# Three early expert jobs after the seventh unit instead of two, and four weight loads moved behind the load of unit 8

## The chip, the cores and the metric

The kernel runs on one core of a Trainium2 chip. The metric is the device time of one execution in microseconds (us); lower is better. The engines are named as the profile names them: PE is TensorE (PEld its weight loads), DVE is VectorE, ACT is ScalarE, POOL is GpSimd, SP is SyncE. A "q" behind an engine's name (SPq, ACTq) marks its sequencer, which issues transfers.

## The reference

A gated scan over 4 sequences of 3648 tokens with 256 channels, and then a two-level mixture of experts over the 14592 resulting tokens. There are 4 groups of 4 experts, each expert a pair of matrices 256x1024 and 1024x256 with a relu between them; a token goes to one expert.

```python
sig = 1.0 / (1.0 + np.exp(-f_logit))
f = lower_bound + (1.0 - lower_bound) * sig
for t in range(S):
    h = f[:, t] * h + (1 - f[:, t]) * x[:, t]
    y[:, t] = h
# y, as N x 256, is the input x of the experts
g_idx = argmax(x @ w_group); g_w = softmax(x @ w_group)[g_idx]
e_idx = argmax(xg @ w_expert[g]); e_w = softmax(xg @ w_expert[g])[e_idx]
out[token] = g_w * e_w * (relu(xg @ w1[g, e]) @ w2[g, e])
```

## The kernel before

**Units.** The tokens are worked off in 29 units of 512 (the last has 256), numbered from 0, so "unit 8" is the ninth. `p1_load` (L174) brings a unit's 1 MB into one of four `zt` buffers; the loads of units 0 to 8 are issued by SP and those from unit 9 on by ACT (`ZX_SP = 9`). ACT computes the gate (tanh L184, affine L194), DVE the gated input (L210, L230) and the scan (`h`, L221, two per unit), PE the transposes back to rows (L248) and the router's logits (L262, L273). After each group of units (`GROUPS`: unit 0, units 1-2, 3-4, 5, 6, then pairs) the routing runs: DVE operations L283 to L377 with the exponential on ACT (L370 up to unit 6, L311 later), and at its end POOL scatters the group's rows, one transfer for 128 rows (L343), into the expert lists `xs` in HBM.

**Jobs.** An expert's tokens go through one early job ("A", in expert order) and one late job ("B", largest first). Early job e is described by `EARLY[e] = (u, n)`: when the units below u are routed, its last 128*n rows (or all, if there are fewer) are loaded from the list (`job_rows`, L750, by SP, behind the scatters). What is left of each expert goes into the late jobs, whose sizes in rows are fixed by `CAPS`, the largest first; a loop at the end takes rows above the caps. For a list that is too short at its cut, SP writes blank rows ahead of it (`early_blanks`, L534, 258 KB for n = 2), two units ahead of the cut's loads. `close_early` (L542, L544) notes what has been taken.

A job has four weight pieces of 512 KB (`job_weights`, L758, on SP, eight staging buffers), each split into a high and a low part (`job_split`: ACT cast L764, DVE subtraction L765); its rows are transposed (L805) and split (L810, L811); the first product runs on L839 to L841 (three matmuls for each block, relu and split on ACT L844 and DVE L845) and the second on L858, scaled on ACT L870 and scattered to the output by POOL (L871).

**Order.** All unit work is cut into 422 small steps (`thunks`), with a mark where a cut is reached: mark 7 at step 126, "begun" at 136, mark 9 at 181, mark 11 at 208, mark 13 at 235. Up to "begun" the steps and the first job's preparation are in the order written. In that stretch the weight pieces are placed by `EARLY_FETCH`: `(5, 4)` puts the first four pieces (job 0) behind the load of unit 5, `(7, 8)` the next four (job 1) behind the load of unit 7, all on SP, which issues strictly in the order written.

```python
for u, n in EARLY_FETCH:
    while u not in last_load:
        bg_pop()
    fetch_to(n)
```

After "begun" the jobs run one behind the other, and unit steps are put between their parts at a rate given by due times. A job of 256 rows counts 10 pieces of work (eight column blocks and two output tiles). The mark that job k+2 needs is due when half of job k is done; before job k+1 begins at PE, its own mark must have been reached. Within these priorities a planner with costs of its own orders each engine's instructions; SP keeps the written order.

```python
nxt = macros[mi + 2][0]
due.append((at - work(mac) // 2, marks[EARLY[nxt.idx][0]] if nxt.kind == "A" else marks["order"]))
```

Two places of the written order matter below. The load of unit 8 comes in SP's order behind the loads of units 6 and 7, the two blanks for cut 9, and job 1's four weight pieces. And in ACT's order the tanh of unit 8 stands ahead of the exponential and the row copies of unit 6's routing, which is the last routing before cut 7; then come the scatters of unit 6, and the loads of the rows for cut 7.

Of the kernel before, what the change touches and what calls it, by code (L numbers as in the profile page):

```python
# [19 lines left out]
NE = 16  # L20
UNIT = 512

EARLY = [(7, 2), (7, 2), (9, 2), (9, 2), (11, 2), (11, 2), (13, 3), (15, 3),
         (15, 3), (17, 4), (19, 4), (21, 4), (23, 5), (25, 5), (27, 6), (27, 6)]
CAPS = [848, 748, 724, 592, 588, 560, 528, 488, 464, 460, 448, 420, 392, 296, 168, 112]
EXTRA_AT = []
GROUPS = [1, 2, 2, 1, 1] + [2] * 11
LAG = 7
EARLY_FETCH = [(5, 4), (7, 8)]
STG_BUFS = 8  # L30
XR_BUFS = 6
ROW_BUFS = 6
# [2 lines left out]
AHEAD = 3  # L35
MT = -(-max(CAPS) // 128)
ZX_SP = 9
# [3 lines left out]
def gated_scan_moe(ctx: ExitStack, tc, zx, lower, wroute, wexp, out, S):  # L41
# [7 lines left out]
    NT = N // P  # L49
    PRE = max(n for _, n in EARLY) * P  # L50
    LW = PRE + N + 2 * P
# [34 lines left out]
    def iota_f32(name, shape, pattern, base=0, mult=0):  # L86
        t = const.tile([P] + shape, F32, name=name)
        nc.gpsimd.iota(t, pattern=pattern, base=base, channel_multiplier=mult,
                       allow_small_or_imprecise_dtypes=True)
        return t  # L90
# [6 lines left out]
    nc.gpsimd.tensor_copy(taken, eoff)  # L97
    cuts = {u for u, _ in EARLY}
    eidx = iota_f32("eidx", [NE], [[1, NE]])
# [97 lines left out]
    def p1_ta(u):  # L197
        p1_tanh(u)
        p1_affine(u)
# [186 lines left out]
    def p1_thunks(us, groups):  # L386
# [21 lines left out]
        def put(f):  # L408
            th.append(f or (lambda: None))
            if hasattr(f, "mark"):  # L410
                marks[f.mark] = len(th)

        put(lambda: [p1_load(u) for u in range(us[0], us[0] + AHEAD - 1)])
        put(lambda: p1_ta(us[0]))
        cut = EARLY[0][0]

# [12 lines left out]
        for u in us + [us[-1] + 1]:  # L429
# [58 lines left out]
            for t in seq:  # L488
                put(t)
                slot += 1  # L490
                for _ in range(2 if u <= EARLY[0][0] else 1):
                    if not hold:
# [37 lines left out]
    def early_blanks(u):  # L530
        for e, (v, n) in enumerate(EARLY):
            if v == u:
                r = e * LW + PRE - n * P
                sync.dma_start(out=xs_v[NT + e][r:r + n * P, :].rearrange("(p k) c -> p k c", k=n),  # L534
                               in_=blank[:, None, :].broadcast_to([P, n, RW]))

    def close_early(u):
        posA = rt.tile([P, NE], I32, name="posA")
        for n in sorted({m for v, m in EARLY if v == u}):
            es = [e for e, s in enumerate(EARLY) if s == (u, n)]  # L540
# [119 lines left out]
    for s in range(NE):  # L660
        nc.vector.memset(caps[:, s:s + 1], float(CAPS[s]))
    onesf = const.tile([P, NE], F32, name="onesf")
# [8 lines left out]
    def make_job(kind, idx):  # L671
        j = Job()
        j.kind, j.idx = kind, idx
        j.len = EARLY[idx][1] * P if kind == "A" else CAPS[idx] if kind == "B" else P
        j.tiles = -(-j.len // P)
# [297 lines left out]
    with tc.manual_schedule(engines={mybir.EngineType.PE, mybir.EngineType.DVE, mybir.EngineType.Activation}):  # L973
        for u, n in EARLY_FETCH:
            while u not in last_load:
# [99 lines left out]
```

## Time and profile before

| | |
|---|---|
| median of 3 runs | 781.0 us (780.71 to 781.51) |
| the profiled execution | 782.62 us |
| its span, first to last instruction | 780.9 us |
| PE busy in the span | 712.0 us (91%) |
| DVE busy | 538.5 us (69%) |
| ACT busy | 460.0 us (59%) |
| POOL busy | 289.7 us (37%) |
| mean granted TensorE clock | 0.964 |

The shares are means over stages that differ much: in the first 70 us there is nothing but unit work; then unit work and early jobs run side by side until all units are routed (about 281 us); then only jobs are left.

### The profile page before, as it was taken

Reading aid. Unit: us, or ns where it says so; the run is one execution under the profiler, and the core shown is the slowest. Engines: PE = TensorE matmul, PEld = TensorE weight load, DVE = VectorE, ACT = ScalarE, POOL = GpSimd, SP = SyncE. Lnnn points to the kernel's source line nnn. Section 1 sums busy time; section 2 is a strip of 40 time slices with the busy share of each in tenths; the row PEclk is TensorE's granted clock in tenths of the full one; section 3 lists DMA queues with packets and bytes.
Section 4 is the critical chain, followed back from the end, with each engine's and each line's share of the span. In section 5 each row is a group of like instructions: output and inputs, shape, how many; then the busy total and the mean of one; then the engine's idle time right before and its main releaser. Section 6 shows DMA issues by size and latency. Waiting matters only on the chain.

```text
span 780.9 us, 20863 instructions
## 1 busy us (share of the span) xinstructions
PE 712.0 (91%) x8112; PEld 631.9 (81%) x8112; DVE 538.5 (69%) x1058; ACT 460.0 (59%) x824; POOL 289.7 (37%) x272
## 2 busy tenths in 40 slices
PE   2653759999999989999999999999999999999995
PEld 1432547888988878889988898999999999999995
DVE  6869999999999976675654645546554676666640
ACT  6558767987878855445445445454455465555541
POOL 3662163677556453552112212223232222222232
PEclk9955969999999999999999999999999999999998
DMA  7997989899999935359355433553554465555300
GB/s 274 345 360 223 359 242 370 302 337 337 310 344 304 364 121 185 121 185 256 121 135 108 148 90 113 142 124 116 136 161 112 145 170 170 153 168 175 88 30 25
DMA packets 96005, 155.58 MB, mean 199 GB/s; under 512 B 52320, under 2 KB 64637, under 8 KB 92576
## 3 DMA queue, kind: packets, MB, share of 16 engines
q1 hardware_dynamic: 80928, 103.73, 45.0%
q0 software_dynamic: 11424, 30.02, 11.2%
q10 hardware_dynamic: 3552, 20.48, 7.2%
q8 instruction: 64, 1.05, 0.6%
q14 instruction: 37, 0.30, 0.1%
HBM read 112.69 MB, written 42.02 MB: 198 GB/s over the span
## 4 chain that ended last, share of the span: by engine, by line
PE 61%; DMA 10%; DVE 9%; issue 5%; ACT 3%; POOL 2%; SPq 1%; POOLq 0%; ACTq 0%; DVEq 0%
PE ps_m L858 29%; PE ps_m L839 7%; PE ps_m L840 7%; PE ps_m L841 7%; DVE wl L765 3%; PE ps_p L839 3%; PE ps_p L841 3%; PE ps_p L840 3%; DMA xs<-rows,posi 3%; DMA xr<-xs 2%; DVE h L221 2%; POOL out_dram L871 2%; DMA zt<-in_zx_dram 2%; DVE hl L845 1%; DMA out_dram<-o,meta 1%
## 5 line engine op out<-in xcount | busy, mean ns | idle before, releaser
L858 PE MATMUL ps_m<-wh,hh 128*128 128x256 f16 (+2 forms) x1320 | 265.8, 252 | 2.8 <-ACT hh L844 2.8
L858 PE MATMUL ps_m<-wh,hl 128*128 128x256 f16 (+2 forms) x1320 | 265.7, 251 | 1.7 <-DVE hl L845 1.6
L858 PE MATMUL ps_m<-wl,hh 128*128 128x256 bf16 (+2 forms) x1320 | 266.0, 251 | 0.1
L858 PEld LDWEIGHTS <-hh 128*128 128x128 f16 (+2 forms) x2640 | 195.6, 99 | 26.5 <-issue 3.3
L839 PE MATMUL ps_m<-xh,wh 128*128 128x256 f16 (+11 forms) x782 | 195.9, 261 | 3.5 <-DVE hl L845 3.5
L840 PE MATMUL ps_m<-xl,wh 128*128 128x256 bf16 (+11 forms) x782 | 196.1, 260 | 0.0
L841 PE MATMUL ps_m<-xh,wl 128*128 128x256 f16 (+11 forms) x782 | 195.9, 260 | 0.0
L765 DVE TENSOR_TENSOR wl<-st,wh 128x1024 bf16<-128x1024 f32 x128 | 154.1, 1217 | 51.4 <-ACT wh L764 51.2
L343 POOL DMA_INDIRECT xs<-rows,posi x114 | 132.9, 1166 | 126.5 <-issue 51.9
L871 POOL DMA_INDIRECT out_dram<-o,info x75 | 87.0, 1161 | 241.6 <-ACT o L870 213.3
L845 DVE SCALAR_TENSOR_TENSOR hl<-ps_m,hh 128x512 bf16<-128x512 f32 (+6 forms) x176 | 117.1, 668 | 73.4 <-ACT hh L844 72.9
L844 ACT ACTIVATE hh<-ps_m 128x512 f16<-128x512 f32 (+6 forms) x176 | 103.6, 590 | 73.0 <-PE ps_m L841 71.4
L764 ACT CAST wh<-st 128x1024 f16<-128x1024 f32 x128 | 132.3, 1048 | 13.9 <-PE ps_m L858 7.7
L840 PEld LDWEIGHTS <-wh 128*128 128x128 f16 x1088 | 106.9, 98 | 12.2 <-issue 4.6
L839 PEld LDWEIGHTS <-wh 128*128 128x128 f16 x1088 | 106.8, 98 | 10.6 <-issue 1.8
L858 PEld LDWEIGHTS <-hl 128*128 128x128 bf16 (+2 forms) x1320 | 104.5, 99 | 12.5 <-DVE hl L845 2.1
L841 PEld LDWEIGHTS <-wl 128*128 128x128 bf16 x1088 | 106.7, 98 | 7.8 <-issue 0.2
L871 POOL DMA_INDIRECT out_dram<-o,meta x55 | 65.3, 1188 | 115.7 <-ACT o L870 105.2
L870 ACT ACTIVATE o<-ps_m,info 128x256 f32<-128x256 f32 (+4 forms) x75 | 33.0, 441 | 84.3 <-PE ps_m L858 77.0
L839 PE MATMUL ps_p<-xh,wh 128*128 128x256 f16 (+13 forms) x306 | 73.3, 252 | 0.0
L840 PE MATMUL ps_p<-xl,wh 128*128 128x256 bf16 (+13 forms) x306 | 73.3, 252 | 0.0
L841 PE MATMUL ps_p<-xh,wl 128*128 128x256 f16 (+13 forms) x306 | 73.3, 252 | 0.0
(145 smaller groups left out, 738.2 us busy)
## 6 DMA issues: line engine op xcount, KB each, us to landing
st<-in_wexp_dram SPq DMA_DIRECT2D x128, 512.0 KB, 6.4
zt<-in_zx_dram ACTq DMA_DIRECT2D x19, 1024.0 KB, 9.4
zt<-in_zx_dram SPq DMA_DIRECT2D x7, 1024.0 KB, 10.0
xr<-xs SPq DMA_DIRECT2D x25, 258.0 KB, 4.9
xs<-blank SPq DMA_DIRECT2D x22, 258.0 KB, 4.6
xs<-rows,posi POOLq DMA_INDIRECT x114
xs<-blank SPq DMA_DIRECT2D x3, 516.0 KB
xs<-blank SPq DMA_DIRECT2D x2, 774.0 KB, 17.7
```

The lines of the kernel that those rows point to most:

```text
L221: nc.vector.tensor_tensor_scan(out=h[:, k, c0 - a:c1 - a], data0=ff[:, k, c0 - a:c1 - a], data1=uu[:, k, c0 - a:c1 - a], initial=init, op0 ...
L343: sc = nc.gpsimd.indirect_dma_start(out=xs_v[G["t0"] + t][:, :], out_offset=bass.IndirectOffsetOnAxis(ap=R["posi"][:, t:t + 1], axis=0), i ...
L764: nc.scalar.copy(j.wh[i], j.st[i])
L765: nc.vector.tensor_tensor(out=j.wl[i], in0=j.st[i], in1=j.wh[i], op=ALU.subtract)
L839: nc.tensor.matmul(po, w1_at(j.wh, k, c), xh[:, k], start=(k == 0), stop=False)
L840: nc.tensor.matmul(po, w1_at(j.wh, k, c), xl[:, k], start=False, stop=False)
L841: nc.tensor.matmul(po, w1_at(j.wl, k, c), xh[:, k], start=False, stop=(k == KD - 1))
L844: nc.scalar.activation(hi, pv, AF.Relu)
L845: nc.vector.scalar_tensor_tensor(out=j.hl[ch][:, cs[0]:cs[-1] + 1, 0:w], in0=pv, scalar=0.0, in1=hi, op0=ALU.max, op1=ALU.subtract)
L858: nc.tensor.matmul(pm[i * q:i * q + n, 0:dw], h[ch][:, c, ts], w2_at(w, c)[:, i * dw:(i + 1) * dw], start=(c == 0 and s == 0), stop=(c == ...
L870: nc.scalar.activation(o[s, 0:dw], pm[s, 0:dw], AF.Copy, scale=lt.bitcast(F32)[s, r, 1:2])
L871: nc.gpsimd.indirect_dma_start(out=out_v[out_n[0]].rearrange("n (g d) -> (n g) d", g=g), out_offset=bass.IndirectOffsetOnAxis(ap=lt[s, r, ...
```

## The change

Expert 2's early job moves from cut 9 to cut 7 and expert 4's from cut 11 to cut 9. So cut 7 feeds three jobs, cut 9 two (experts 3 and 4) and cut 11 one (expert 5); the number of rows that a job works on stays 256. The caps of the late jobs in slots 3 to 6 are set anew (592, 588, 560, 528 become 616, 592, 588, 548). And job 1's four weight pieces are issued behind the load of unit 8 instead of that of unit 7.

```diff
-EARLY = [(7, 2), (7, 2), (9, 2), (9, 2), (11, 2), (11, 2), (13, 3), (15, 3),
+EARLY = [(7, 2), (7, 2), (7, 2), (9, 2), (9, 2), (11, 2), (13, 3), (15, 3),
          (15, 3), (17, 4), (19, 4), (21, 4), (23, 5), (25, 5), (27, 6), (27, 6)]
-CAPS = [848, 748, 724, 592, 588, 560, 528, 488, 464, 460, 448, 420, 392, 296, 168, 112]
+CAPS = [848, 748, 724, 616, 592, 588, 548, 488, 464, 460, 448, 420, 392, 296, 168, 112]
 EXTRA_AT = []
 GROUPS = [1, 2, 2, 1, 1] + [2] * 11
 LAG = 7
-EARLY_FETCH = [(5, 4), (7, 8)]
+EARLY_FETCH = [(5, 4), (8, 8)]
```

## Rows read from the trace of the kernel before

**Rows 1.** The page's second part: busy tenths of PE and DVE in 40 equal slices of the span (19.5 us each).

```profile
PE   2653759999999989999999999999999999999995
DVE  6869999999999976675654645546554676666640
```

**Rows 2.** Busy time of the engines by stretch: from:to, length, busy us (instructions) of PE, PEld, DVE, ACT and POOL, granted clock, share of the DMA engines, GB/s.

```profile
18.00:62.00 44.00, 24.07 (x186) 16.62 (x186) 32.97 (x77) 25.94 (x57) 28.16 (x25) 0.78 0.97 327
62.00:130.00 68.00, 44.25 (x389) 34.71 (x390) 65.49 (x104) 50.69 (x93) 23.90 (x21) 0.77 0.91 296
130.00:281.00 151.00, 147.53 (x1536) 130.69 (x1534) 146.17 (x272) 121.22 (x228) 90.52 (x71) 1.00 0.98 325
281.00:736.00 455.00, 454.50 (x5385) 412.97 (x5383) 267.45 (x536) 234.82 (x402) 129.25 (x116) 1.00 0.51 144
```

**Rows 3.** Timeline of ACT ahead of cut 7: start, length, what; in brackets the idle time before it and what ended it. The tanh at 38.32 is that of unit 6, the one at 57.46 that of unit 8, and 58.58 is unit 8's affine step; 61.03 is the last of unit 6's routing.

```profile
38.32 1.06 ACT L184 ACTIVATE zt<-zt 128x1024 f32<-128x1024 f32 x1 [3.37 <-DMA zt<-in_zx_dram]
50.44 0.23 ACT L274 COPY Lg<-ps_p 128x80 f32<-128x80 f32 x1 [0.42 <-PE ps_p L273]
57.46 1.06 ACT L184 ACTIVATE zt<-zt 128x1024 f32<-128x1024 f32 x1 [6.80 <-DMA zt<-in_zx_dram]
58.58 1.50 ACT L194 ACTIVATE zt<-zt,mid,half 128x512 f32<-128x512 f32 x2
61.03 0.17 ACT L379 COPY runoff<-ps_p 128x16 f32<-128x16 f32 x1
```

**Rows 4.** Timeline of DVE in the same stretch and a little behind it: the scans of unit 4, the first operation of unit 6's routing behind the exponential, the scan of unit 7 behind cut 7, the gated input of unit 9, and the four weight subtractions of job 0.

```profile
30.34 2.47 DVE L221 TENSOR_TENSOR_SCAN h<-zt,h 128x512 f32<-128x512 f32 x2
58.71 0.23 DVE L315 TENSOR_REDUCE sm<-ex 128x20 f32<-128x80 f32 x1 [5.74 <-ACT ex L370]
61.58 0.34 DVE L221 TENSOR_TENSOR_SCAN h<-zt,h 128x64 f32<-128x64 f32 x1
66.44 1.19 DVE L210 SCALAR_TENSOR_TENSOR zt<-zt 128x1024 f32<-128x1024 f32 x1
72.62 4.61 DVE L765 TENSOR_TENSOR wl<-st,wh 128x1024 bf16<-128x1024 f32 x4
```

**Rows 5.** Timeline of SP's issues: start, length from the first issue of a line to its last, what. Behind 18.76 (blanks for cut 7), 20.18 (job 0's pieces) and 23.95 (units 6 and 7) come 29.63 (blanks for cut 9), 30.88 (job 1's pieces) and 38.37 (unit 8). The last row is from SP's waits up to 60 us: who waited for whom, us in total, times, longest.

```profile
18.76 1.38 SPq L534 DMA_DIRECT2D xs<-blank  x2
20.18 3.65 SPq L758 DMA_DIRECT2D st<-in_wexp_dram  x4
23.95 5.63 SPq L174 DMA_DIRECT2D zt<-in_zx_dram  x2
...
29.63 1.21 SPq L534 DMA_DIRECT2D xs<-blank  x2
30.88 4.90 SPq L758 DMA_DIRECT2D st<-in_wexp_dram  x4
38.37 0.33 SPq L174 DMA_DIRECT2D zt<-in_zx_dram  x1
...
SPq L174 <- DMA zt<-in_zx_dram: 2.5, 1, 2.5
```

**Rows 6.** DMA packets in four stretches, in this order: 23 to 26, 38 to 42, 42 to 48 and 48 to 57 us. A blank's packet has 1032 bytes, a weight piece's 4096, a scatter's 4128, that of a unit from unit 2 on 8192 (128 of them, the only ones not under 8 KB); the counts are cumulative, and those under 512 B carry no data of these.

```profile
DMA packets 593, 0.79 MB, mean 264 GB/s; under 512 B 52, under 2 KB 529, under 8 KB 584
DMA packets 657, 1.25 MB, mean 311 GB/s; under 512 B 73, under 2 KB 503, under 8 KB 616
DMA packets 642, 1.95 MB, mean 325 GB/s; under 512 B 106, under 2 KB 188, under 8 KB 641
DMA packets 925, 3.69 MB, mean 410 GB/s; under 512 B 161, under 2 KB 320, under 8 KB 672
```

**Rows 7.** ACT's issue of the load of unit 9, and that transfer's time from issue to landing.

```profile
48.73 0.34 ACTq L174 DMA_DIRECT2D zt<-in_zx_dram  x1
...
DMA to landing us min/median/max: 11.4/11.4/11.4
```

**Rows 8.** Timeline of POOL: the first scatter of units 3 and 4, the last of unit 5, the first and the last of unit 6; those between follow each other at 1.28 us.

```profile
42.15 1.20 POOL L343 DMA_INDIRECT xs<-rows,posi  x1 [2.23 <-ACT zt L194]
56.48 0.97 POOL L343 DMA_INDIRECT xs<-rows,posi  x1 [0.30 <-issue]
60.93 0.97 POOL L343 DMA_INDIRECT xs<-rows,posi  x1 [3.47 <-ACT rows L252]
65.27 0.97 POOL L343 DMA_INDIRECT xs<-rows,posi  x1 [0.30 <-issue]
```

**Rows 9.** The chain of work that ended last, about cut 7 and cut 9 (start, us, what), and the first of PE's waits from 60 to 140 us (us in total, times, longest).

```profile
70.85 2.62 DMA xr<-xs
...
108.87 5.17 DMA xr<-xs
...
PE ps_p L805 <- DMA xr<-xs: 12.7, 2, 6.4
```

**Rows 10.** The same chain among the late jobs. The pieces of L858 are second products; between one that ends and the next that begins lies a first product, of 208 rows ahead of 553.56 and of 144 rows ahead of 626.58. x48 is two output tiles of 128 rows; x120 (of 120 matmuls) is one tile of 128 rows and one of at most 32.

```profile
544.04 5.24 PE ps_m L858 x48
553.56 2.62 PE ps_m L858 x24
...
618.34 5.24 PE ps_m L858 x48
626.58 2.62 PE ps_m L858 x24
...
634.44 3.53 PE ps_m L858 x120
```

## Prediction

> **What bounds the kernel now.** I read the page first, then windows by stage, and then the timelines of the stretch that the change touches. The digits of PE and DVE [rows 1] show three stages: PE has gaps up to slice 7, DVE is full from slice 4 to 15, and from slice 15 on PE is full and DVE is not. The windows [rows 2] put numbers to it. From 281 to 736 us PE is busy for 454.50 of 455 us at the full clock: there only PE's work counts, and every microsecond added to it is added to the end. From 62 to 281 us DVE is the fuller engine: 65.49 of 68 and 146.17 of 151 us, 7.3 us idle in 219. PE is idle for 23.8 us from 62 to 130, at a mean clock of 0.77, but for only 3.5 us from 130 on. The reader is to see that PE's holes before 130 are not holes of the kernel: DVE works right through them. From 18 to 62 us no engine is full (DVE 32.97 of 44) while the DMA engines are (0.97).
>
> Ahead of cut 7 the timelines show what DVE waits for. ACT sits idle twice for a unit's data: 3.37 us for unit 6 and 6.80 us for unit 8 [rows 3]. The second wait is odd: unit 8 isn't needed for cut 7, but its tanh stands in ACT's order ahead of the exponential of unit 6's routing, and DVE waits 5.74 us for that [rows 4]. So a load that nobody needs yet holds up the routing that closes the cut. Why it is late is in SP's queue [rows 5, 6]. Unit 8 is issued at 38.37, behind job 1's four pieces, and then moves behind them too: from 42 to 48 us one packet of 8 KB moves (642 less 641), from 48 to 57 us 253 (925 less 672), which is all of units 8 and 9. From 42 to 48 the queue is at the 4 KB packets of job 1.
>
> **Part 1: the late jobs, certain loss.** An early job takes what its list holds at the cut, at most 256 rows. Counting with the reference on its inputs, expert 2 has 188 tokens in units 0 to 6 (244 in units 0 to 8), and expert 4 has 236 below unit 9 (256 or more below unit 11). So 56 and 20 rows fall back to late jobs; the slots' loads become 608, 584, 577 and 539, all within the new caps, so the loop at the end stays empty. The caps rise by 616+592+588+548 less 592+588+560+528, 76 rows. First product: 553.56 less 549.28 is 4.28 us for 208 rows, 626.58 less 623.58 is 3.00 for 144, hence 0.020 us for a row and 76 x 0.020 = 1.5 us. Second product: the 528 slot ended in a full tile and one of at most 32 rows, 3.53 us; the 616 slot ends in 128 and 104 rows, as two full tiles 5.24 us; the other three keep their kind of tail. 5.24 - 3.53 = 1.7. Sum **3.2 us** [rows 10], on an engine with 0.5 us idle in 455 [rows 2]: nothing hides it. The early jobs stay at 256 rows, so PE gets nothing back.
>
> **Part 2: one blank more for cut 7, one less for cut 11.** The third blank (258 KB) goes into SP's queue ahead of job 0's pieces and unit 6. From 23 to 26 us 477 of the two blanks' 512 packets moved, 2.6 us for two, so 1.3 for one [rows 6]. ACT and through it DVE and POOL wait for unit 6 already [rows 3, 8], so all up to unit 6's routing comes **1.3 us later**. The bound below is nothing (0.65 us if only SP's issue counted). The missing blank for cut 11 moved behind unit 8 and held up nobody that the trace names.
>
> **Part 3: unit 8 ahead of job 1's pieces, the gain.** SP can issue unit 8 once its buffer is free. That buffer was unit 4's, whose last scan ends at 32.81 [rows 4], and its place in the queue is then right behind the blanks for cut 9, whose packets are through by about 43. (The last 2.5 us of its wait today are for an earlier unit's load to land [rows 5]; if that wait stays, it is issued at 38.4 as now and still ahead of its turn.) With 1.3 us for the new blank and 3.4 to 5.6 us for 1 MB (an estimate: at the 311 GB/s of 38 to 42 us, and at 60% of it) it lands at 48 to 50. ACT reaches the tanh at 50.67 + 1.3 = 52.0 [rows 3]: it waits no more. 57.46 - 52.0 is 5.4 us for ACT. What is late next? DVE has its part of the routing done 5.74 us ahead of 58.71, at 53.0, and with 1.3 it is 54.3: it gains 4.4. The row copies wait for PE's transposes, which follow DVE, so unit 6's routing ends on ACT at about 57.1 instead of 61.03, and DVE goes on with unit 7's scan at 57.6 instead of 61.58: **3.9 us**. POOL gains less: its last scatter of unit 5 starts at 56.48, now 57.8, and the next can start 1.28 us later at 59.1 instead of 60.93; four of them at 1.28 end their issue from 62.9 instead of 65.27, so job 0's rows come **2.4 us** earlier [rows 8, 9]. Since DVE has 11 us of unit work between that scan and job 0's weights [rows 4], the 3.9 hold if units 9 and 10 come in time.
>
> Unit 9 is the check. Job 1's pieces now move while it does. Issued at 50.0 and with the 11.4 us of its row it lands at 61.4 [rows 7]; tanh and affine take 2.6 [rows 3], so its gated input starts at 64.0, where an advance of 3.9 asks for 62.5. That costs 1.5 and leaves 2.4. The Trainium skill (DMA: Bandwidth & Descriptors, "Queues, rings and completion order") says that each DMA engine goes round robin between the queues that have work, packet by packet. By that rule unit 9 gets, by an estimate, a third of the 410 GB/s of 48 to 57 us with three queues working, 1 MB in 7.7 us, lands at 58 and costs nothing; the row, in which two other queues worked too, took 11.4 us. By the rule the sum below would be 0.6 us better, by the row 0.9 worse. I take **3.3 us** for parts 2 and 3, between 2.4 and 3.9.
>
> Job 1's pieces come some 6 us later than now, about 56, and are split behind 72.6 [rows 4]: hidden by job 0's weights.
>
> **Part 4: the third job.** PE waits 12.7 us for rows, half of it (6.35) up to 114, when job 2's land, which cut 9 yields [rows 9]. With cut 7 that wait goes. The due times change with it: mark 9 was due at half of job 0, 45 steps of unit work for 5 pieces of work; now it is due at half of job 1, 3 steps for each piece instead of 9. Job work moves forward, unit work back, and from job 5 on the order stands where it stood. But each job of 256 rows also needs DVE: 4.61 us for its weights [rows 4], and more for its rows and first product. The order up to job 5 holds the same DVE work as before, and DVE was idle for 2.5 us of the 68 [rows 2]. So PE's 6.35 us are worth at most those 2.5, and 4.8 more only if the idle time from 130 to 281 goes too. Below, it can be nothing, if job chains (PE, ACT, DVE, PE) leave DVE idle where unit work filled it. I take **1.7 us**, nearer to the 2.5, as the wait itself is gone.
>
> **Sum.** 3.2 - 3.3 - 1.7 = -1.8 us. The profiled execution took 782.62 us (span 780.9 and 1.7 around it), so 780.8 by its own time; it lies 1.6 above the median of the runs, so **779.2** as a median. The measurement of this kernel can tell about 0.2% (1.6 us) from no change, so this is near the edge.
>
> **Rivals.**
> - *PE's idle time is worth what it says.* Job 2 fills the hole, and DVE's lulls from 130 to 281 close with it, because they stem from PE being late. For it: 23.8 us of PE idle at clock 0.77 [rows 2]. Against: DVE at 96 and 97%. Up to 3.3 + 7.3 - 3.2, 7.4 us faster; with half of the lulls in question 3.5. Time 773.6 to 777.8.
> - *Unit 9 takes unit 8's place (slower).* ACT's wait moves from unit 8's tanh to unit 9's, because the same bytes have to pass engines that are full from 18 to 62 us [rows 2]. Its gated input starts at 66.44 today [rows 4]; if unit 9 lands after 63.8, everything gained at unit 8 is given back, and the blank's 1.3 and the caps' 3.2 stay: 781.0 + 3.2 + 0 to 1.3, less at most 1 of part 4, 783.2 to 785.5. For it: 11.4 us for that load today, with less behind it. It needs 2.4 us more than that.
> - *It doesn't do what it says.* POOL's 2.4 count, job 2's rows are there, but DVE's order leaves the same idle time: 3.2 - 2.4 to 3.0 = 0.2 to 0.8 slower, 781.2 to 781.8.
>
> **How the numbers follow.** My case (DVE-bound, gain of 3.2 to 6.4 before the caps, 777.8 to 781.0) gets 0.50, the first rival 0.20, the slower one 0.17, the last 0.13. Faster by over 0.2% means below 779.4: half of my case and the first rival, 0.47. Slower means above 782.6: the second rival and a little, 0.18. The rest is 0.35. The range leaves out two fifths of the first rival and some two thirds of the second: 775.3 to 784.0; my case alone is 777.8 to 781.0.
>
> **What the profile after would show.** ACT's 6.80 us wait ahead of unit 8's tanh gone, and that of unit 6 grown from 3.37 to about 4.7; DVE's operation behind the exponential at about 54; the first scatter of unit 6 at 59; the rows for cut 7 loaded three times at about 68.5; no PE wait for rows but the one for job 0; DVE still over 95% busy from 60 to about 275; PE full from there, some 3 us longer. I am wrong if unit 9's tanh waits past 63, if DVE's idle time from 62 to 281 changes by more than 3 us, or if the stretch of the late jobs grows by another sum than 3.2.

## The result, and the profile after

The changed kernel takes 786.66 us (median of 11 runs, 784.52 to 791.84); the kernel before takes 781.67 beside it (11 runs). The ratio is 1.0061, with a 95% interval of 1.0043 to 1.0080: slower by 5.0 us. I had predicted 779.2, and 784.0 as the upper end. In the medians of the experiments below, runs that lie over 1.5% above the fastest of their kernel are left out.

The profiled execution took 788.97 us, 6.35 more than that of before. The windows of the changed kernel, in the columns of [rows 2]:

```profile
18.00:62.00 44.00, 23.90 (x188) 16.77 (x186) 32.58 (x74) 25.62 (x58) 26.39 (x23) 0.59 0.99 315
62.00:130.00 68.00, 50.92 (x454) 41.59 (x455) 64.57 (x110) 53.82 (x96) 29.63 (x25) 0.79 0.91 302
130.00:281.00 151.00, 141.72 (x1455) 124.26 (x1455) 144.19 (x261) 118.75 (x221) 90.49 (x71) 0.99 0.97 320
281.00:736.00 455.00, 452.41 (x5224) 411.62 (x5222) 268.44 (x532) 233.33 (x398) 129.23 (x115) 1.00 0.51 144
```

From 62 to 130 PE does 6.7 us more than before: job 2 fills the hole as meant. From 130 to 281 it does 5.8 less, and DVE, the fuller engine, does 0.9 and 2.0 less: 2.9 us of its work are missing by 281.

Ahead of cut 7, ACT's timeline shows a wait gone and another grown. The rows are the tanh of unit 6, the tanh of unit 8, the last copy of unit 6's routing and the tanh of unit 9:

```profile
44.23 1.06 ACT L184 ACTIVATE zt<-zt 128x1024 f32<-128x1024 f32 x1 [9.04 <-DMA zt<-in_zx_dram]
...
56.65 1.06 ACT L184 ACTIVATE zt<-zt 128x1024 f32<-128x1024 f32 x1
...
61.61 0.18 ACT L379 COPY runoff<-ps_p 128x16 f32<-128x16 f32 x1
63.35 1.06 ACT L184 ACTIVATE zt<-zt 128x1024 f32<-128x1024 f32 x1 [1.56 <-DMA zt<-in_zx_dram]
```

Unit 8's wait of 6.80 us [rows 3] is gone: from unit 6's tanh to unit 8's it is now 12.42 us, where it was 19.14. But unit 6's tanh starts 5.91 us later (44.23, was 38.32), for its wait grew from 3.37 to 9.04. The two nearly cancel: the routing of unit 6 ends at 61.61 instead of 61.03.

The reason for the first is in the DMA packets. Kernel before, 26 to 30 us, and then the changed kernel, 23 to 26 and 26 to 30 us (the first stretch of before is in [rows 6]):

```profile
DMA packets 401, 1.32 MB, mean 329 GB/s; under 512 B 55, under 2 KB 90, under 8 KB 400
```

```profile
DMA packets 543, 0.76 MB, mean 254 GB/s; under 512 B 54, under 2 KB 486, under 8 KB 523
DMA packets 498, 0.83 MB, mean 207 GB/s; under 512 B 46, under 2 KB 382, under 8 KB 497
```

Packets of 512 B to 2 KB are the blanks. In the first three microseconds 432 moved, fewer than the 477 of before; the rest took up to 30 us (336 more), and in that time the engines moved 0.83 MB instead of 1.32. From 30 to 34 us it is 1.24 MB instead of 1.60, so that by 34 us 0.88 MB less have moved since 23. Job 0's pieces and unit 6 stand behind the blanks in SP's order and come later. At the 401 GB/s of before's 30 to 34 us, the missing 0.88 MB and the blank's own 0.26 are some 2.8 us (an estimate); what the rest of the 5.91 is isn't shown.

POOL's scatters pass the delay on. The first of units 3 and 4, the first of unit 6, and the last; then SP's issue of the rows for cut 7:

```profile
48.06 1.20 POOL L343 DMA_INDIRECT xs<-rows,posi  x1 [7.89 <-ACT zt L194]
...
63.70 1.81 POOL L343 DMA_INDIRECT xs<-rows,posi  x1 [0.30 <-DMA xs<-rows,posi]
...
69.42 1.02 POOL L343 DMA_INDIRECT xs<-rows,posi  x1 [0.30 <-issue]
```

```profile
72.65 2.63 SPq L750 DMA_DIRECT2D xr<-xs  x3
```

The first is 5.91 us later than in [rows 8], just as much as unit 6's tanh, and from there POOL runs without a gap: with it they are 16 scatters, mostly 1.28 us apart up to the first of unit 6, the last four 2.1, 1.3 and 2.3 us apart. Job 0's rows are issued at 72.65, not at 70.85 [rows 9].

How far the jobs are is read from the split of their rows (DVE, L811). First the kernel before, then the changed kernel: job 0, job 1, job 5, job 6 (the first with three tiles), job 8.

```profile
77.14 0.68 DVE L811 TENSOR_TENSOR xl<-ps_p,xh 128x512 bf16<-128x512 f32 x1
100.97 0.68 DVE L811 TENSOR_TENSOR xl<-ps_p,xh 128x512 bf16<-128x512 f32 x1
161.45 0.68 DVE L811 TENSOR_TENSOR xl<-ps_p,xh 128x512 bf16<-128x512 f32 x1
174.82 0.41 DVE L811 TENSOR_TENSOR xl<-ps_p,xh 128x256 bf16<-128x256 f32 x1
207.60 0.41 DVE L811 TENSOR_TENSOR xl<-ps_p,xh 128x256 bf16<-128x256 f32 x1
```

```profile
78.44 0.68 DVE L811 TENSOR_TENSOR xl<-ps_p,xh 128x512 bf16<-128x512 f32 x1
90.97 0.68 DVE L811 TENSOR_TENSOR xl<-ps_p,xh 128x512 bf16<-128x512 f32 x1
158.06 0.68 DVE L811 TENSOR_TENSOR xl<-ps_p,xh 128x512 bf16<-128x512 f32 x1
175.75 0.41 DVE L811 TENSOR_TENSOR xl<-ps_p,xh 128x256 bf16<-128x256 f32 x1
211.53 0.42 DVE L811 TENSOR_TENSOR xl<-ps_p,xh 128x256 bf16<-128x256 f32 x1
```

Job 0 is 1.3 us behind, job 1 10.0 us ahead of before, job 5 3.4 ahead, job 6 0.9 behind, job 8 3.9 behind. So the lead that the third job brings is real and is given back by job 6: from job 0 to job 6 it takes 97.31 us, where it took 97.68. What is lost, 3.0 us, is lost between jobs 6 and 8. The windows of that stretch, from split to split, before and changed:

```profile
174.82:207.60 32.78, 32.42 (x372) 28.84 (x371) 32.61 (x68) 26.79 (x52) 20.59 (x16) 1.00 1.01 335
175.75:211.53 35.78, 34.75 (x378) 31.09 (x378) 33.00 (x68) 26.00 (x49) 18.73 (x17) 0.95 0.95 314
```

DVE carries out 68 instructions in both, but it is idle for 2.8 us instead of 0.2. PE's waits, from 60 to 140 and from 140 to 215 us in the changed kernel, and from 140 to 215 in the kernel before:

```profile
PE ps_p L805 <- DMA xr<-xs: 7.1, 1, 7.1
PE ps_m L839 <- DVE hl L845: 3.2, 2, 1.8
```

```profile
PE ps_m L839 <- DVE hl L845: 4.9, 4, 1.8
PE ps_p L805 <- DMA xr<-xs: 1.4, 2, 0.8
```

```profile
PE ps_m L839 <- DVE hl L845: 0.2, 1, 0.2
```

The wait for job 2's rows is gone (12.7 twice [rows 9], now 7.1 once). In its place PE waits longer for DVE than before.

Last the late jobs. The first matmul of the first tail of 208 rows, and the last output of a slot near the end; kernel before, then the changed kernel:

```profile
461.98 0.25 PE L839 MATMUL ps_p<-xh,wh 128*128 128x208 f16 x1
715.58 0.47 ACT L870 ACTIVATE o<-ps_m,info 128x256 f32<-128x256 f32 x1 [1.78 <-issue]
```

```profile
465.73 0.25 PE L839 MATMUL ps_p<-xh,wh 128*128 128x208 f16 x1
722.43 0.47 ACT L870 ACTIVATE o<-ps_m,info 128x256 f32<-128x256 f32 x1 [1.78 <-issue]
```

3.75 us behind at the one, 6.85 at the other: the new caps cost 3.10.

### The profile page after: what moved, and what is told of

The parts are those of the page before. It is cut to its first block, busy times and chain, and to the rows that moved or that the text cites. A ratio compares the mean times of both kernels' runs of the same rounds, so it can differ in the third digit from the quotient of the medians.

```text
span 787.2 us, 20696 instructions
## 1 busy us (share of the span) xinstructions
PE 717.4 (91%) x8040; PEld 637.3 (81%) x8040; DVE 539.3 (69%) x1053; ACT 462.1 (59%) x824; POOL 293.4 (37%) x272
## 4 chain that ended last, share of the span: by engine, by line
PE 52%; issue 11%; DVE 10%; DMA 10%; POOL 4%; ACT 2%; SPq 1%; POOLq 0%; DVEq 0%; ACTq 0%
PE ps_m L858 26%; PE ps_m L839 6%; PE ps_m L841 6%; PE ps_m L840 6%; DMA xs<-rows,posi 4%; DVE wl L765 4%; PE ps_p L839 3%; PE ps_p L841 3%; PE ps_p L840 3%; DMA st<-in_wexp_dram 2%; POOL out_dram L871 2%; DVE h L221 2%; POOL xs L343 2%; DMA zt<-in_zx_dram 1%; DVE hl L845 1%
## 5 line engine op out<-in xcount | busy, mean ns | idle before, releaser
L858 PE MATMUL ps_m<-wh,hl 128*128 128x256 f16 (+3 forms) x1296 | 266.7, 252 | 0.1
L858 PE MATMUL ps_m<-wl,hh 128*128 128x256 bf16 (+3 forms) x1296 | 266.5, 252 | 0.1
L858 PE MATMUL ps_m<-wh,hh 128*128 128x256 f16 (+3 forms) x1296 | 266.4, 253 | 0.0
L858 PEld LDWEIGHTS <-hh 128*128 128x128 f16 (+3 forms) x2592 | 196.3, 100 | 23.1 <-issue 3.3
L839 PE MATMUL ps_m<-xh,wh 128*128 128x256 f16 (+10 forms) x782 | 198.2, 262 | 13.5 <-DVE hl L845 10.5
L840 PE MATMUL ps_m<-xl,wh 128*128 128x256 bf16 (+10 forms) x782 | 198.6, 262 | 0.0
L841 PE MATMUL ps_m<-xh,wl 128*128 128x256 f16 (+10 forms) x782 | 198.5, 262 | 0.0
L858 PEld LDWEIGHTS <-hl 128*128 128x128 bf16 (+3 forms) x1296 | 104.6, 100 | 10.0 <-issue 0.2
L870 ACT ACTIVATE o<-ps_m,info 128x256 f32<-128x256 f32 (+4 forms) x75 | 33.3, 443 | 84.3 <-PE ps_m L858 75.6
L839 PE MATMUL ps_p<-xh,wh 128*128 128x256 f16 (+11 forms) x306 | 73.8, 253 | 0.0
L840 PE MATMUL ps_p<-xl,wh 128*128 128x256 bf16 (+11 forms) x306 | 73.7, 252 | 0.0
## 6 DMA issues: line engine op xcount, KB each, us to landing
xs<-blank SPq DMA_DIRECT2D x22, 258.0 KB, 11.9
```

The costliest lines, as they stand in the source:

```text
L839: nc.tensor.matmul(po, w1_at(j.wh, k, c), xh[:, k], start=(k == 0), stop=False)
L840: nc.tensor.matmul(po, w1_at(j.wh, k, c), xl[:, k], start=False, stop=False)
L841: nc.tensor.matmul(po, w1_at(j.wl, k, c), xh[:, k], start=False, stop=(k == KD - 1))
L858: nc.tensor.matmul(pm[i * q:i * q + n, 0:dw], h[ch][:, c, ts], w2_at(w, c)[:, i * dw:(i + 1) * dw], start=(c == 0 and s == 0), stop=(c == ...
L870: nc.scalar.activation(o[s, 0:dw], pm[s, 0:dw], AF.Copy, scale=lt.bitcast(F32)[s, r, 1:2])
```

## The experiments

They ran on four chips (B to E), on which the kernel before takes 816 to 823 us. That the result ran on a fifth, called A here, is taken from its time of 781.67; no number of that chip is known. Every run is compared with the kernel before on its own chip. The differences are those of the medians. The ratio is an estimate of its own and not the quotient of these medians; where the two differ (due_again, late_old, hole_fetch), its interval says what can be told.

| kernel | chip | before, us | difference, us | ratio, 95% interval |
|---|---|---|---|---|
| caps_only | B | 817.07 | +2.05 | 1.0005 to 1.0037 |
| fetch_only | B | 817.07 | -0.04 | 0.9980 to 1.0026 |
| jobs_only | B | 817.07 | +11.71 | 1.0118 to 1.0175 |
| blank_late | B | 817.07 | +8.07 | 1.0077 to 1.0158 |
| after_again | C | 822.72 | +8.49 | 1.0052 to 1.0127 |
| fetch_again | C | 822.72 | +0.52 | 0.9964 to 1.0026 |
| blank_early | C | 822.72 | +0.98 | 0.9990 to 1.0062 |
| due_old | C | 822.72 | +2.75 | 0.9994 to 1.0059 |
| due_again | D | 821.98 | +5.16 | 1.0054 to 1.0111 |
| late_old | D | 821.98 | +2.13 | 0.9971 to 1.0033 |
| blank_hole | D | 821.98 | -4.58 | 0.9901 to 0.9959 |
| hole_fetch | D | 821.98 | -4.46 | 0.9938 to 1.0012 |
| after_third | E | 816.26 | +11.86 | 1.0078 to 1.0155 |
| after_hole | E | 816.26 | +3.68 | 1.0022 to 1.0080 |
| after_hole_old | E | 816.26 | -2.06 | 0.9944 to 1.0004 |
| hole_again | E | 816.26 | -5.91 | 0.9901 to 0.9956 |

On these chips the change as a whole costs 8 to 12 us (after_again, after_third), not 5. The theories that the expectations name: A, the third blank is what I mis-sized; B, the new order of the loads is to blame or its gain is swallowed; C, the due times that come with the third job are to blame; D, there is a gain left when both are out.

### One part at a time: caps, load order, jobs

The kernel before with the new `CAPS` alone:

> The kernel before with only the new caps, so that the late jobs in slots 3 to 6 work on 76 rows more than they need. Both theories: 3.2 us slower than before (1.5 of first products, 1.7 of second ones), all of it between the late jobs of slots 3 and 6; up to 281 us nothing changes. If the time rises by under 2 or over 4.5 us, the sum of the certain loss was wrong too.

+2.05 us, 0.4 to 3.0 by the interval: a little under the 3.10 of the rows above, and under the 3.2 that were expected.

The kernel before with the weight pieces of job 1 behind unit 8, twice:

```diff
-EARLY_FETCH = [(5, 4), (7, 8)]
+EARLY_FETCH = [(5, 4), (8, 8)]
```

> The kernel before with only job 1's weight pieces moved behind the load of unit 8; jobs, blanks and caps as before. Theory A (the third blank is what was mis-sized; the order of the loads is a gain): unit 6's tanh stays at 38.3 us, unit 8's tanh no longer waits (6.80 us before), the first scatter of unit 6 starts at 57.8 to 59 instead of 60.93, the rows for cut 7 come 2 to 3 us earlier; the time is 777.5 to 779.5, 2 to 4 us under the kernel before. Theory B (unit 8 in the queue behind unit 6 is what made unit 6 late): unit 6's tanh at 42 to 44 as in the changed kernel, time 783 to 785.

> Job 1's pieces behind unit 8, nothing else changed; a second measurement, to see whether the stall of 7.9 us on all engines at 51 to 59 us belongs to this kernel. Theory A (the order of the loads is a gain of its own): 1 to 4 us faster than before, rows for cut 7 at 67 to 69 us. Theory B (the whole gain is taken by something else that is late in the same stretch): within 1 us of before, rows at 70 us or later.

No change, both times. Unit 8 comes without a wait for its data, but on these chips PE, ACT and DVE stand still at that place, while POOL's scatters go on. In the fences, "issue" is time in which the engine waited for nothing that the profile shows, and "remote" a wait whose end has no record in the trace. Timeline of PE in fetch_only, of ACT in it, and of PE in caps_only, which has the old order:

```profile
59.72 0.47 PE L273 MATMUL ps_p<-ident,rs 128*128 128x128 f32 x1 [7.87 <-issue]
```

```profile
59.40 0.27 ACT L265 COPY rs<-ps_p 128x128 f32<-128x128 f32 x1 [7.88 <-remote]
```

```profile
61.43 0.47 PE L273 MATMUL ps_p<-ident,rs 128*128 128x128 f32 x1 [10.02 <-ACT rs L265]
```

The pause stands where the 6.80 us were to be gained; the trace names no data that it waits for. In the profile of the kernel before on the first chip ACT waits there for unit 8. So what the new order is worth alone on that chip is not measured.

The changed kernel without the new load order:

> The changed kernel with job 1's weight pieces back behind the load of unit 7; three jobs at cut 7, three blanks and the new caps stay. Theory A: unit 6's tanh at about 44 as in the changed kernel, and unit 8's tanh waits again, some 5 to 7 us; the cut comes later than in the changed kernel; 788 to 792. Theory B: unit 6's tanh at 39 to 40 and the time at 783 to 786, under the changed kernel.

+11.71 us, as dear as the whole change is on chip E, and unit 6 is as late as in the changed kernel, so the load order did not make it late. That is against B. The tanh of unit 6 in caps_only and in jobs_only:

```profile
40.01 1.06 ACT L184 ACTIVATE zt<-zt 128x1024 f32<-128x1024 f32 x1 [5.36 <-DMA zt<-in_zx_dram]
```

```profile
44.58 1.06 ACT L184 ACTIVATE zt<-zt 128x1024 f32<-128x1024 f32 x1 [9.57 <-DMA zt<-in_zx_dram]
```

### The blank

The changed kernel with expert 2's blank sent later, with those of cut 11:

```diff
-            if v == u:
+            if (11 if e == 2 else v) == u:
```

> The changed kernel with expert 2's blank issued with that of expert 5, two units' loads and job 1's pieces later, so that two blanks stand ahead of unit 6's load as before. Theory A: unit 6's tanh back at 38 to 39 (44.2 in the changed kernel), rows for cut 7 loaded at 67.5 to 69 (72.65), time 780 to 783, 4 to 6 us under the changed kernel. Theory B: unit 6's tanh still at 42 to 44, time as the changed kernel, 785.5 to 787.5.

Unit 6's tanh is back at 40.20, yet the kernel is still 8.07 us slower. Theory A's 780 to 783 us would have been within 2 us of the kernel before. The blank makes unit 6 late, as A said, but that is not the larger part of the loss.

The kernel before with the blanks moved as in the change and nothing else:

```diff
-            if v == u:
+            if {2: 7, 4: 9}.get(e, v) == u:
```

> The kernel before with the blanks alone moved: expert 2's goes out with those of cut 7, expert 4's with those of cut 9; jobs, caps and the order of the weight loads are as before. Theory A (the blank is what was mis-sized): unit 6's tanh 4 to 6 us later, and as much later the rows for cut 7; 3 to 5 us slower than before. Theory C (what costs time is the third job's place in the order, and the early stretch absorbs a late unit 6): unit 6 is as late, but the kernel is within 1.5 us of before.

Unit 6's tanh is at 44.02, where fetch_again on the same chip, with two blanks (and the new order of the loads), has it at 39.64: 4.4 us for one blank. In all the profiles of these chips with the blanks of cut 7 in their place, it starts at 43.35 to 45.78 with three blanks (six profiles) and at 39.64 to 41.73 with two (five). The kernel is 0.98 us slower, but the interval goes from 0.8 faster to 5.1 slower: it rules out neither C's 1.5 nor A's 3 to 5. In these two profiles 3.0 us of the delay are still there at job 8 (219.6 against 216.6) and none at 322 us, as C said; that is one execution of each.

### The due times

The changed kernel with the due times as they were, twice:

```diff
-due.append((at - work(mac) // 2, marks[EARLY[nxt.idx][0]] if nxt.kind == "A" else marks["order"]))
+due.append((at - work(mac) // 2, marks[{2: 9, 4: 11}.get(nxt.idx, EARLY[nxt.idx][0])] if nxt.kind == "A" else marks["order"]))
```

> The changed kernel with the due times of the unit work left as they were (mark 9 due at half of job 0, mark 11 at half of job 2), so that job 2 can start early but unit work isn't put behind it. Theory A (the due times move nothing for good): within 1.5 us of the changed kernel. Theory C (unit work that was put off for job 2 is what is missing from 130 us on): 2 to 5 us faster than the changed kernel, PE's wait for rows between job 1 and job 2 gone all the same. Theory D (the early lead is worth something at the end): 1 to 3 us slower than the changed kernel.

> The changed kernel with the due times of the unit work left as they were, a second measurement. Theory C (the put-off unit work is the larger part of the loss): within 0.2 to 0.5% of the kernel before, that is the caps and about 1 us for the blank. Theory A (the blank is the larger part): 0.6% or more slower than before.

5.7 us faster than the changed kernel on chip C (2.75 instead of 8.49; the intervals of the two overlap a little), as C said. On D it is 5.16 us slower than before, 0.5 to 1.1% by the interval, where C had 0.2 to 0.5 and A 0.6 or more: by its own terms the second run speaks for the blank as the larger part. The changed kernel wasn't run on D. Windows from 130 to 281 us, the changed kernel (after_again) and due_old:

```profile
130.00:281.00 151.00, 134.15 (x1305) 111.05 (x1298) 129.95 (x246) 104.95 (x197) 81.77 (x68) 0.95 0.95 304
```

```profile
130.00:281.00 151.00, 143.02 (x1436) 123.55 (x1436) 141.39 (x262) 115.23 (x212) 86.82 (x72) 0.98 1.00 323
```

With the new due times DVE does 11.4 us less and PE 8.9 less in this stretch. Where it goes shows in the split of the rows: job 1, job 6 and job 8 of after_again, and then of due_old:

```profile
97.47 0.68 DVE L811 TENSOR_TENSOR xl<-ps_p,xh 128x512 bf16<-128x512 f32 x1
184.38 0.41 DVE L811 TENSOR_TENSOR xl<-ps_p,xh 128x256 bf16<-128x256 f32 x1
226.63 0.41 DVE L811 TENSOR_TENSOR xl<-ps_p,xh 128x256 bf16<-128x256 f32 x1
```

```profile
113.96 0.68 DVE L811 TENSOR_TENSOR xl<-ps_p,xh 128x512 bf16<-128x512 f32 x1
188.49 0.41 DVE L811 TENSOR_TENSOR xl<-ps_p,xh 128x256 bf16<-128x256 f32 x1
221.86 0.41 DVE L811 TENSOR_TENSOR xl<-ps_p,xh 128x256 bf16<-128x256 f32 x1
```

A lead of 16.5 us at job 1 (3.0 of them there already at job 0, 85.57 against 88.58) is one of 4.1 at job 6 and 4.8 behind at job 8: from job 6 to job 8 it takes 42.2 us with the new due times, 33.4 with the old. It is the shape of the first chip's rows, larger. The windows from the split of job 6 to that of job 8, of after_again and due_old:

```profile
184.38:226.63 42.25, 39.39 (x411) 32.85 (x411) 33.29 (x68) 28.74 (x56) 19.33 (x17) 0.93 0.91 298
188.49:221.86 33.37, 33.17 (x377) 29.44 (x375) 32.79 (x68) 26.88 (x53) 19.60 (x16) 1.00 1.00 338
```

DVE does the same work, 68 instructions, and is idle for 9.0 us instead of 0.6. All the profiles of these chips divide the same way: with the new due times (jobs_only, blank_late, after_again, after_third, after_hole) it takes 40.0 to 42.2 us from job 6 to job 8, with the old ones (the other eleven) 33.3 to 34.1, whatever the blanks and the loads do; DVE is idle in it for 6.7 to 9.0 us in the five and for at most 1.3 in the eleven. From job 0 to job 6 it takes 98 to 103 us with either. So the loss lies there and comes with the due times, but the work that was put off isn't itself what is missing: by job 6 it has been made up. In each of the five ACT has two waits in or just ahead of that stretch whose end has no record, of 3.3 to 5.5 us ahead of L810 and of 2.8 to 3.7 ahead of L265, and PE's second products stand with "issue"; none of the eleven has these two. On the first chip neither kernel has them.

Both suspects out (late blank, old due times):

> The changed kernel with both suspects taken out: expert 2's blank goes out with those of cut 11, and the due times are the old ones. What is left of the change is the order of the loads, job 2's earlier rows and the caps. Theory C: 2 to 3 us slower than before, which is the caps alone. Theory D (there is a gain of its own in the order of the loads and in job 2's rows): 1 us slower to 3 us faster than before.

+2.13 us, with an interval from 2.4 faster to 2.7 slower: no difference from before is shown, the caps' 2 would fit, and D isn't ruled out. Against due_again on the same chip, the late blank saves 3.0 us by the medians, and the two intervals lie apart. The order of the loads and job 2's earlier rows bring no gain that shows.

### The blanks in the gap of the queues

Before unit 5's load can be issued, SP waits for its buffer, and the queues run empty: 12 packets from 17 to 19 us. The kernel before with the two blanks of cut 7 ahead of that load, twice:

```diff
-put(lambda u=u: (p1_load(u + AHEAD - 1), early_blanks(u + 4)))
+put(lambda u=u: (u == 3 and early_blanks(7), p1_load(u + AHEAD - 1), u > 3 and early_blanks(u + 4)))
```

> The kernel before with the two blanks of cut 7 issued ahead of unit 5's load, where the queues move nothing from 17 to 19 us. Theory A (a blank in the crowded stretch is worth its time to the end): unit 6's tanh 2 to 4 us earlier, ACT's wait for it gone, and 2 to 3 us faster than before. Theory C (the early stretch is worth little at the end): unit 6 is as much earlier, but the kernel is within 1 us of before.

> The kernel before with the two blanks of cut 7 in the gap of the queues, a second measurement: 0.4 to 0.9% faster than before, if the first one holds; within 0.2% if its 5 us were the scatter of the runs.

4.58 and 5.91 us faster than before, more than the 2 to 3 of theory A: faster than both kernels. SP issues the blanks at 10.2 us there, not at 18.76 [rows 5]. Packets from 17 to 19 us, before and in hole_again, then unit 6's tanh in blank_hole:

```profile
DMA packets 12, 0.04 MB, mean 20 GB/s; under 512 B 7, under 2 KB 7, under 8 KB 7
```

```profile
DMA packets 389, 0.46 MB, mean 228 GB/s; under 512 B 30, under 2 KB 377, under 8 KB 377
```

```profile
36.23 1.06 ACT L184 ACTIVATE zt<-zt 128x1024 f32<-128x1024 f32 x1
```

Unit 6 comes without a wait. Taking two blanks out of the crowded stretch is worth 5 to 6 us at the end, while putting one in cost 1 us that can't be told from nothing (nor from 5); whether these are unequal, and why, is open.

As the last one, and with the blanks of cut 9 sent with those of cut 11 and job 1's pieces behind unit 8:

> As the last one, and besides the blanks of cut 9 go out with those of cut 11, behind unit 8's load, and job 1's weight pieces behind unit 8. Jobs, caps and due times are as before. Theory A: unit 6 and unit 8 without a wait, rows for cut 7 by 4 us or more earlier, 3 to 6 us faster than before. Theory C: rows 4 us earlier, the kernel within 1.5 us of before.

-4.46 us, and by the interval from 5.1 faster to 1.0 slower: nothing beyond blank_hole that shows.

The changed kernel beside the same edit, without and with the old due times:

> The changed kernel, unaltered, beside the other three. 0.6 to 1.2% slower than the kernel before.

> The changed kernel with the three blanks of cut 7 issued ahead of unit 5's load, where the queues are empty; due times as in the change. Unit 6's tanh at 36 to 38 us without a wait. If the blank's price is the larger part of the loss: 5 us or more faster than the changed kernel, and not slower than before by more than the caps' 2 to 3. If the due times are the larger part: 2 to 4 us faster than the changed kernel and still 4 us or more slower than before.

> As the last one, and with the old due times of the unit work. If the due times cost 3 us or more, it is that much faster than the last one, and within 0.3% of the kernel before or faster. If they cost nothing, it takes the time of the last one within 1.5 us.

All on chip E. after_hole is 8.2 us faster than the changed kernel, as was expected if the blank's price is the larger part, and still 3.68 slower than before (1.8 to 6.5 by the interval), which lies between the two expectations: neither suspect is the whole loss. Together with C and D these runs give a table of both suspects (us against before):

| | new due times | old due times |
|---|---|---|
| blanks of cut 7 in their place | +8.5, +11.9 | +2.8, +5.2 |
| blanks of cut 7 in the gap | +3.7 | -2.1 |

The due times cost 5.7 us in the first line (chip C) and 5.7 in the second (chip E, where the intervals lie apart); the place of the three blanks costs 8.2 in the first column (chip E). after_hole_old is 3.9 us slower than hole_again: the three jobs, the third blank, the caps and the new order of the loads together bring a loss even then, of which the caps alone are 2 to 3.

## Why the prediction was wrong, point by point

**Part 1, the caps: right on the first chip.** 3.2 us predicted, 3.10 by the rows. Measured alone on chip B it is 2.05 (0.4 to 3.0), so 3.2 is a little too much there.

**Part 2, the third blank: mechanism right, price wrong.** "2.6 us for two, so 1.3 for one" took the fastest stretch in [rows 6] and bounded it only from below. Even that row gives more: 477 packets in three microseconds are 3.2 us for 512, 1.6 for one blank. The same rows showed a slower stretch: 430 packets of cut 9's blanks took the four microseconds from 38 to 42, by which one blank's 256 take 2.4. Unit 6's tanh came 5.9 us later, and 4.4 in the run that moves the blanks alone. The step that failed is the blank's price: it was taken from one good stretch, and the load behind the blank was charged with the blank's own time alone. The slowest row would have been nearer, and still short by 2 us or more.

**Part 3, the load order: right in itself on the first chip.** I had ACT gain 6.8 us between the two tanh (6.72 measured) and the routing of unit 6 end 3.9 us earlier with the blank's 1.3 in it, 5.2 without; 5.91 less 0.58 is 5.3. With the blank's true price nothing is left of it, and the rows come 1.8 us later instead of 2.4 earlier. This is read from one pair of profiles; the runs of the order alone show no gain, on chips where another pause stands in that place.

Unit 9 was no obstacle: DVE does its gated input at 67.06, right behind the scan of unit 8. Its load was issued at 54.64 and its tanh started at 63.35 after a wait of 1.56, so it landed some 8.7 us after its issue, where 11.4 was the row [rows 7]. The Trainium skill (DMA: Bandwidth & Descriptors, "Queues, rings and completion order"), by whose round robin I had worked out, as an estimate, a landing at 58 after an issue at 50.0, agrees better with that than the row does.

**Part 4, the third job: wrong in sign.** "PE's 6.35 us are worth at most those 2.5", "Below, it can be nothing". PE's wait is gone, and job 1 is 10.0 us ahead. But I bounded the effect by nothing on the side of the loss and took the idle time of DVE from 62 to 281 as given. It rose from 7.3 to 10.2 us, nearly all of it between jobs 6 and 8 (0.2 to 2.8), and between job 0 and the late jobs the kernel lost 2.45 us (1.3 behind at job 0's split, which came at 78.44 instead of 77.14, and 3.75 at the late jobs) instead of gaining 1.7. On the other chips the due times alone cost 5.7, twice. Counting the written order, 160 unit steps are done when job 2 comes up instead of 192; they are made up by job 6 (248 and 252). Up to there nothing is lost, and nothing gained either: job 6 comes 97.31 us behind job 0, in the kernel before 97.68. With DVE full, job 2's early start moved work and saved none, so that nothing of the 1.7 came.

Why DVE goes idle between jobs 6 and 8 isn't settled. The written order there is again nearly that of before. In the changed kernel PE runs at a granted clock of 0.60 (a mean over its two levels, 1.2 and 2.4 GHz) from 175.7 to 180.0, right behind a wait of 1.85 us for DVE; in the kernel before it was 1.00 then. Windows of these 4.3 us, before and changed:

```profile
175.70:180.00 4.30, 4.30 (x73) 3.94 (x71) 4.30 (x15) 4.30 (x8) 2.94 (x2) 1.00 1.02 376
```

```profile
175.70:180.00 4.30, 4.00 (x38) 3.80 (x38) 4.03 (x13) 2.03 (x4) 2.33 (x3) 0.60 1.02 390
```

PE gets through 38 matmuls instead of 73 there, 31 of the first products instead of 45. That may delay the routing work that DVE waits for some 10 us later (1.5 us for ACT's copy of the logits, behind PE, at 190.8). No run separates it from the rest. On the other chips the loss is larger, and the waits without a record that stand there are a rival to the put-off work as its cause: the new order may only move such a pause onto DVE's path.

**The sum.** -1.8 was predicted for the profiled execution, +6.35 measured, 8.15 apart. 4.6 of it is the state at job 0's split (1.3 behind instead of 3.3 ahead), as much as the blank cost more than I had priced it at (5.9 instead of 1.3). 4.15 is the third job with its due times (2.45 lost instead of 1.7 gained), less 0.1 at the caps and 0.5 behind the last slots. Of the 1.3 behind, 0.6 are there at unit 7's scan (62.17, was 61.58), and most of the rest comes with unit 10, whose tanh waits 2.07 us for its load. The rival that ended slower had the time nearly right (783.2 to 785.5) by the wrong mechanism, which is luck. Two figures of the forecast don't add up, and nothing hangs on them: half of my case and the first rival are 0.45, not 0.47, and 3.5 us faster than 781.0 is 777.5, not 777.8.

Of the signs that I had named, unit 9's tanh did wait past 63 us, and that wait was harmless; DVE's idle time changed by 2.9 us, inside the 3 that I had allowed, and that was not harmless. The sign that spoke earliest was one that I had put a number to: unit 6's wait, 9.04 instead of 4.7.

## What to carry to other kernels

When a transfer goes into queues that are already full, price it by the slowest stretch in which the trace shows it, not the fastest, and take even that as the least that the load behind it loses (2.4 us by the rows here, 4 to 6 measured); and look first for a place where the queues are empty. An early start that pushes other work back gains nothing when both need the same full engine, and isn't free: bound it on the side of the loss too, by the idle time that the new order may cause later. Check which other decisions hang on a number in a table (here the due times on the cut of a job) and try them apart.

## What the hardware showed that I had not expected

The same kernel takes 781.7 us on one chip and 816 to 823 on four, a difference that no run explains. On the second kind PE is busy for some 440 us from 281 to 736 instead of 454 at nearly the same clock (some records of PE can be missing), its waits there are mostly put down to "issue", and ahead of cut 7 fourteen of the sixteen profiles show a pause of 5 to 12 us on PE, between the router's two products (7.87 and 10.02 above), for which the trace names no transfer. A gain that depends on that stretch can be there on one chip and not show on another; the losses of this change were larger on the second kind.

256 packets of 1032 B (258 KB) in a full queue put off the load behind them by 4.4 us (chip C) and 5.9 (A), while from 23 to 26 us 477 such packets had moved in three.
